# Empty pieces between the products of logits, an opening in another order, and the second head's key copies on VectorE

## The chip, the cores and the metric

The kernel runs on one core of a Trainium2 chip. The metric is the device time of one execution in microseconds (us). Engines go by the names of the profile: PE (TensorE matmul; PEld its weight loads), DVE (VectorE), ACT (ScalarE), POOL (GpSimd) and SP (SyncE, which issues most DMAs). L120 is line 120 of the kernel before. Each engine works through its own instructions in program order, and the kernel sets that order by hand.

## The reference

Attention with two window masks, and a mixture of experts on its output. Shapes: q, k, v are (8, 8, 576, 64); the experts see x of (4608, 512), with 8 experts of 512 x 1024.

```
scores = q @ k^T / 8                      # per batch and head
rel = i - j
plain:   0 <= rel < 32                    # heads 0 to 3
dilated: 0 <= rel < 128 and rel % 4 == 0  # heads 4 to 7
attn = softmax(where(mask, scores, -1e9))
x = (attn @ v), heads side by side        # (4608, 512)

do = x @ w_skip > 0                       # rows that go to an expert
logits = x @ w_gate ; e = argmax ; g = softmax(logits)[e]
out = x + do * g * (relu(x @ w1[e]) @ w2[e])
```

## The kernel before, in words

**Attention in 24 steps.** A quad is two batches and four heads of one kind (plain or dilated); there are 8 quads of 3 parts, so 24 steps. `Attention.run` writes each step's instructions in the order of the string `STEP`, letter by letter, and every engine then keeps that order. Step t works on several steps at once: `A` is the weighted sum (attention times v, L184) of step t, `T` the transposes of the weights (L172) of t+1, `E` the exponential (L157) of t+2, `R` the products of scores (L139) and the three `S` the shift of t+3: add the mask on DVE (L147), row maximum on DVE (L151), subtract it on POOL (L153). `D` normalises (L194, L196, L198 on DVE), `X` transposes the finished rows of the step before (L241 on PE, L244 or L251 on ACT). `k0A` and `k1A` copy the keys of t+4.

**Keys.** `place` (L120) copies the 64 partitions of one head of a pair into one of two block-diagonal tiles `kT`; the other half of each head's block is zero, cleared once at the start by `clear` as listed in `CLEAR` (all four on DVE, L105). A product of scores needs both heads' copies, and the one PSUM tile `s` that the mask's add of the step before has read. In the steps both copies are on ACT; in the opening the first is on ACT and the second on DVE.

**Opening.** Before step 0 a loop over t = 0 to 3 writes: copies of t, products of t, all three parts of its shift, the next load, the exponential of t - 1; and last the transposes of step 0.

**Router.** After each pair of batches but the last, `Router.run` is a generator whose pieces turn x into lists of rows for the experts: four products of logits (L509, each of four matmuls per batch half, in `logits`) with a copy by ACT (L511), nine transposes (L521) with reductions on DVE (L523), `choose`, `rank`, `find`, `put` (L664) for rows and for gates, then `listed`. It is started at the second `X` of the first step of the next pair, and each `w` in `STEP` draws one piece; there are 13 `w` per step. For the third pair, the wrapper `early` does more once it hears `listed`: it closes the first expert's list (L489 and the small DVE rows L491 to L742), gathers its first two tiles of rows (L878 on POOL), writes 16 empty pieces, then the transposes of the gathered rows (L896) and the first three products of the expert's hidden layer (L914). What is left of the pieces after step 23 is drained in one go.

**Experts.** After the attention `finish` routes the last pair while the first expert goes on; then seven more experts follow, each with L914 (up) and L984 (down), the weights split into a high and a low part (L805 on ACT, L806 on DVE or POOL).

Of the kernel before, what the change touches and what calls it, by code (L numbers as in the profile page):

```python
# [20 lines left out]
B, H, S, D = 8, 8, 576, 64  # L21
NTOK, DM = B * S, H * D
E, F = 8, 1024
GQ = 64
NG = S // GQ
W = 32
# [41 lines left out]
class Attention:  # L68
# [27 lines left out]
    def clear(self, tile, hh, eng):  # L96

        dst = tile[64 - 64 * hh:128 - 64 * hh, hh]
        if eng == "A":
            n = 3 * 4  # L100
            dst = dst.rearrange("c n x -> c (n x)").rearrange("c (n x) -> c n x", n=n)
            zeros = self.junk[64 - 64 * hh:128 - 64 * hh, 0:dst.shape[2]]
            self.nc.scalar.copy(out=dst, in_=zeros.unsqueeze(1).broadcast_to(list(dst.shape)))
        else:
            {"V": self.nc.vector, "G": self.nc.gpsimd}[eng].memset(dst, 0.0)  # L105

    def load(self, kind, t):

        src = {"q": self.q, "k": self.k, "v": self.v}[kind][t]
        tile = self.kp.tile([P, 4, src.shape[2]], F32, name=kind, bufs=3 if kind == "q" else 2)  # L110
        n = W + GQ * NB if kind == "k" and t // PARTS % 2 == 0 else src.shape[2]
        self.nc.sync.dma_start(out=tile[:, :, 0:n], in_=src[:, :, 0:n])
        return tile[:, :, 0:n] if kind == "k" else tile.rearrange("c (r b) (g y i) -> c r b g y i", r=2, g=NB, y=2)
# [142 lines left out]
    def run(self, router, experts, early, finish):  # L256


        nc = self.nc
        quads = [(bp, half) for bp in range(B // 2) for half in range(2)]  # L260
        steps = PARTS * len(quads)
        ins, diags, xTs, sms, shifts, exps, pend = {}, {}, {}, {}, {}, {}, {}

        def load(kind, t):
            if t < steps:
                ins[kind, t] = self.load(kind, t)

        def product(t):
            if t < steps:
                i, part = divmod(t, PARTS)  # L270
                sms[t], go, shift, exps[t] = self.scores(quads[i][1], ins["q", t], diags["k", t], part)
                go()
                shifts[t] = shift()

        def shift(t):
            next(shifts.get(t, iter(())), None)

        def exp(t):
            if t < steps:
                exps.pop(t)()  # L280

        def place(t, kind, hh, eng):
            if t < steps:
                diags[kind, t] = self.place(kind, t, ins[kind, t], int(hh), eng)


        masks = make_masks(nc, self.kp)
        for kind, t in FIRST:
            load(kind, t)
        nc.vector.memset(self.junk, 0.0)  # L290
        self.maskp = next(masks)
        for op in CLEAR.split():
            self.clear(self.kts[int(op[1])], int(op[2]), op[3])
        make_identity(nc, self.ident)
        self.maskd = next(masks)
        self.warm(WARM)
        def turn(t):
            if t < steps:
                go, *pend[t] = self.weighted(sms.pop(t))
                go()  # L300

        for t in range(4):
            place(t, "k", 0, "A")
            place(t, "k", 1, "V")
            if t < 3:
                product(t)
                for _ in range(3):
                    shift(t)
                load("k", t + 2)
                if t == 1:  # L310
                    load("q", 3)
            if t in (1, 2):
                exp(t - 1)
        turn(0)

        works, news, stores, xp = [iter(())], [], [], []
        for t in range(steps):
            i, part = divmod(t, PARTS)
            bp, half = quads[i]
            g0 = NB * part  # L320
            while stores:
                self.store_rows(*stores.pop())
            for kind, ahead in (("k", 5), ("q", 4), ("v", 2)):
                if (kind, t + ahead) not in FIRST + FOLLOW:
                    load(kind, t + ahead)
            if t == 1:
                self.prepare()
                dil_rows = make_dil_rows(nc, self.consts["pool"])
                next(dil_rows)
            elif t == 2:  # L330
                self.dil_rows = next(dil_rows)
            if t == WSTART - 1:
                experts.open_first()
            if t == WSTART:
                experts.load_next()
            if half == 0 and part == 0 and bp:
                news.append(early(bp - 1, router(bp - 1, xTs[bp - 1])))
            xh = self.xp.tile([P, NB, 256], F32, name="xh", bufs=3)
            sums, divide = pend.pop(t)
            divides = []  # L340
            for op in STEP.split():
                if op == "T":
                    turn(t + 1)
                elif op == "R":
                    product(t + 3)
                elif op == "E":
                    exp(t + 2)
                elif op == "S":
                    shift(t + 3)
                elif op == "A":  # L350
                    sums(ins["v", t])
                    divides.append(divide(xh))
                elif op == "D":
                    next(divides[0])
                elif op == "X":
                    if xp:
                        xp.pop(0)()
                    if not xp and news:
                        works[0] = news.pop()
                elif op == "W":  # L360
                    if t > WSTART:
                        experts.split_first()
                elif op == "w":
                    next(works[0], None)
                else:
                    place(t + 4, *op)
            if half == 0 and part == 0:
                xTs[bp] = self.xp.tile([P, 4, 2, S], F32, name="xT")
            xp = self.transpose_x(xTs[bp], half, xh, g0)
            stores.append((bp, half, xh, g0))  # L370
        for _ in works[0]:
            pass
        self.att_ctx.close()
        finish(xp, bp, xTs[bp], lambda: self.store_rows(*stores.pop()))
# [13 lines left out]
LATER = 8  # L388
WSTART = 16
GATHER = 16  # L390
WARM = 12
FIRST = [("k", 0), ("q", 0), ("k", 1), ("q", 1), ("v", 0), ("q", 2), ("v", 1)]
FOLLOW = [("k", 2), ("k", 3), ("q", 3), ("k", 4)]
CLEAR = "k00V k01V k10V k11V"

STEP = "E A w T w D w R D w D w X w S w X w S w k0A W w W w k1A W w S w W"
CAP = 384
NT = CAP // P
TILES = [NT] * 5 + [NT - 1] * 3
# [427 lines left out]
class Experts:  # L827
# [189 lines left out]
    def finish(self, e, t, w, hs, th, xg, tag="o"):  # L1017
        r, a = self.router, NT * e + t
        return self.down(w, hs, th, xg[:, t], r.write[:, a:a + 1], r.gate[:, a:a + 1], self.views[t], tag)
# [4 lines left out]
    def early_rows(self):  # L1024

        for _ in range(GATHER):
            yield
# [168 lines left out]
def make_dil_rows(nc, const):  # L1196

    pos = const.tile([P, NG], F32, name="pos")
    res = const.tile([P, NG], F32, name="res")
    rows = const.tile([P, B // 2, NG], F32, name="rowsf")  # L1200
    rows_i = const.tile([P, B // 2, NG], I32, name="rowsi")
    for p in range(0, P, W):
        nc.gpsimd.iota(pos[p:p + W], pattern=[[W, NG]], base=0, channel_multiplier=1,
                       allow_small_or_imprecise_dtypes=True)
    yield
    nc.vector.tensor_scalar(out=res, in0=pos, scalar1=float(RL), scalar2=float(4 - 2 * S), op0=ALU.is_ge, op1=ALU.mult)
    nc.vector.scalar_tensor_tensor(out=res, in0=pos, scalar=float(2 * RES), in1=res, op0=ALU.mult, op1=ALU.add)
    for bp in range(B // 2):
        for p in range(0, P, W):
            b, y = divmod(p // W, 2)  # L1210
            nc.vector.tensor_scalar_add(rows[p:p + W, bp], res[p:p + W], float(2 * S * (2 * bp + b) + 2 * y + 1))
    nc.vector.tensor_copy(out=rows_i, in_=rows)
    yield rows_i
# [3 lines left out]
def moe_attention_kernel(ctx: ExitStack, tc: tile.TileContext, q, k, v, w_skip, w_gate, w1, w2, out):  # L1217
    nc = tc.nc

    def early(bp, listing):  # L1220

        for name in listing:
            if name == "listed" and bp == B // 2 - 2:
                router.close_early()
                router.read_list(0, EARLY)
                experts.xg0 = experts.fetch(0, 0, EARLY, rows=NTOK - 2 * S)
                router.write_list(0, EARLY)
            yield
        if bp == B // 2 - 2:
            yield from experts.early_rows()  # L1230
            yield from experts.early_hidden()
# [120 lines left out]
```

## Time and profile before

| | |
|---|---|
| times of 3 runs | 501.49, 502.75 (median), 507.65 us |
| profiled execution, its own time | 501.86 us |
| its span, first to last instruction | 499.8 us |
| mean granted TensorE clock in the span | 0.922 |
| PE, PEld busy | 413.4 us (83%), 343.2 us (69%) |
| DVE, ACT, POOL busy | 273.7 us (55%), 221.7 us (44%), 158.5 us (32%) |
| HBM read, written | 80.27 MB, 14.94 MB (191 GB/s over the span) |

The span falls into an opening (to 25.68 us, where the first weighted sum starts), the 24 steps (to about 217 us), the routing of the last pair beside the first expert (to about 275 us), and the experts. In a row of the timeline the first number is the start, the second the duration, then engine, line, operation, what it writes and reads, its shape and count; in brackets stands how long the engine was idle before it and what ended that wait. "Issue" means that nothing the profile shows was waited for. The ends of matmuls are modelled.

### The profile page before, as it was taken

To read this page: it belongs to the slowest core of one execution; us is meant where nothing else is said; L and a number is where in the kernel's file an instruction comes from. 1 tells how busy PE (TensorE), PEld (TensorE's weight loads), DVE (VectorE), ACT (ScalarE), POOL (GpSimd) and SP (SyncE) were. 2 spreads that over 40 slices of the span, in tenths; PEclk is the share of its full clock that TensorE was granted. 3 is DMA by queue.
4 is the path that set the end of the run, shared out by engine and by line. 5 is a ranking of instruction groups with operands and counts; after the bars stand their busy time and mean duration, and the time that the engine had idled before them with its cause. 6 is when DMAs were issued, how large, how long until landed. Compare 5 with 4: busy or idle time off the path is not lost. (4 is left out here: it accounts for less than half of the span.)

```text
span 499.8 us, 13402 instructions
## 1 busy us (share of the span) xinstructions
PE 413.4 (83%) x5426; PEld 343.2 (69%) x5426; DVE 273.7 (55%) x575; ACT 221.7 (44%) x441; POOL 158.5 (32%) x217
## 2 busy tenths in 40 slices
PE   5576678787966786668779999999999999999980
PEld 3455554665655555556658988988989989797970
DVE  4477343964586439431966464573573665757620
ACT  2265365646655565324325361452452534645500
POOL 3253352248127673262534042301202113030000
PEclk8698798978999789669999999999999999999995
DMA  8469856969697966271075665446256445755000
GB/s 293 156 206 300 284 198 205 337 231 295 226 325 261 352 217 164 90 228 48 1 232 189 225 220 179 140 168 208 85 171 200 138 162 194 244 206 206 21 26 13
DMA packets 44297, 95.50 MB, mean 191 GB/s; under 512 B 5243, under 2 KB 16395, under 8 KB 44224
## 3 DMA queue, kind: packets, MB, share of 16 engines
q1 hardware_dynamic: 38976, 79.08, 47.6%
q0 software_dynamic: 5248, 15.44, 9.1%
q8 instruction: 46, 0.75, 0.6%
q14 instruction: 27, 0.22, 0.1%
HBM read 80.27 MB, written 14.94 MB: 191 GB/s over the span
## 5 line engine op out<-in xcount | busy, mean ns | idle before, releaser
L984 PE MATMUL o<-w,h 128*128 128x512 f32 x320 | 104.3, 400 | 1.5 <-ACT h L917 1.1
L884 POOL DMA_INDIRECT out_dram<-yo,write x21 | 22.6, 1074 | 160.4 <-DVE yo L989 160.4
L914 PE MATMUL s<-xh,w 128*128 128x384 f32 (+1 forms) x236 | 70.3, 313 | 0.0
L139 PE MATMUL s<-kT,q 128*32 128x128 f32 x1152 | 47.8, 319 | 27.1 <-DVE kT L120 10.7
L914 PE MATMUL s<-xl,w 128*128 128x384 f32 (+1 forms) x236 | 70.0, 311 | 0.0
L984 PEld LDWEIGHTS o<-w,h 128*128 128x128 f32 x320 | 59.1, 188 | 13.9 <-ACT h L917 1.5
L153 POOL TENSOR_TENSOR sm<-sm,mx 128x768 f32<-128x768 f32 x24 | 36.6, 1525 | 94.2 <-DVE mx L151 52.4
L139 PEld LDWEIGHTS s<-kT,q 128*32 128x32 f32 x1152 | 38.3, 128 | 34.8 <-issue 24.9
L917 ACT ACTIVATE h<-s 128x384 fp32r<-128x384 f32 (+1 forms) x59 | 26.2, 444 | 81.1 <-issue 35.4
L184 PE MATMUL o<-v,pT 64*32 64x65 f32 x2304 | 37.0, 237 | 17.7 <-issue 14.2
L184 PEld LDWEIGHTS o<-v,pT 64*32 64x32 f32 x2304 | 28.9, 110 | 26.2 <-issue 19.9
L120 ACT COPY kT<-k 64x1024 f32<-64x1024 f32 (+1 forms) x44 | 43.8, 996 | 5.0 <-DMA k<-in_k_dram 4.5
L914 PEld LDWEIGHTS s<-xh,w 128*128 128x128 f32 x236 | 44.6, 189 | 1.3 <-issue 1.0
L914 PEld LDWEIGHTS s<-xl,w 128*128 128x128 f32 x236 | 44.6, 189 | 0.4
L157 ACT ACTIVATE sm<-sm 128x768 f32<-128x768 f32 x24 | 20.3, 845 | 40.7 <-POOL sm L153 40.5
L806 DVE TENSOR_TENSOR w2l<-w2l,w 128x512 fp32r<-128x512 f32 x40 | 27.6, 691 | 18.6 <-ACT w L805 17.1
L226 POOL DMA_INDIRECT out_dram<-xh,rowsi x33 | 33.5, 1014 | 11.9 <-issue 8.6
L878 POOL DMA_INDIRECT xg<-out_dram,read x24 | 24.4, 1018 | 39.3 <-DMA out_dram<-yo,write 15.1
L806 DVE TENSOR_TENSOR w0l<-w0l,w 128x512 fp32r<-128x512 f32 x40 | 27.7, 691 | 15.1 <-ACT w L805 13.5
L918 DVE SCALAR_TENSOR_TENSOR h<-s,h 128x384 fp32r<-128x384 f32 (+1 forms) x59 | 29.0, 491 | 11.3 <-ACT h L917 11.2
L241 PE MATMUL tp<-ident,xh 128*128 128x128 f32 x144 | 25.9, 314 | 8.9 <-ACT pT L173 8.3
L989 DVE SCALAR_TENSOR_TENSOR yo<-o,gate,xg 128x512 f32<-128x512 f32 x21 | 15.7, 750 | 29.5 <-PE o L984 26.6
(203 smaller groups left out, 758.4 us busy)
## 6 DMA issues: line engine op xcount, KB each, us to landing
v<-in_v_dram SPq DMA_DIRECT2D x24, 780.0 KB
w0l<-in_moe_w_dram SPq DMA_DIRECT2D x48, 256.0 KB
w1l<-in_moe_w_dram SPq DMA_DIRECT2D x40, 256.0 KB
w2l<-in_moe_w_dram SPq DMA_DIRECT2D x40, 256.0 KB
q<-in_q_dram SPq DMA_DIRECT2D x24, 384.0 KB
k<-in_k_dram SPq DMA_DIRECT2D x12, 512.0 KB
k<-in_k_dram SPq DMA_DIRECT2D x12, 448.0 KB
out_dram<-xh SPq DMA_DIRECT2D x24, 192.0 KB
```

What stands on the lines that cost most here:

```text
L120: copy(out=to[own, hh, :, 0:tile.shape[2]], in_=tile[own])
L139: nc.tensor.matmul(ps[0][p:p + W, r, 2 * KW * g:2 * KW * (g + 1)], lhsT=q[:, r, b, g, sub], rhs=kT[:, :, r, b, a:a + KW], start=True, stop ...
L153: nc.gpsimd.tensor_tensor(out=rows, in0=rows, in1=mx.broadcast_to([P, 4 * NB, KW]), op=ALU.subtract)
L184: nc.tensor.matmul(ps[0][p:p + W, hh, y * m:y * (m + 1)], lhsT=pT[own, NB * r + g, p:p + W], rhs=v[own, r, b, g, sub], start=True, stop=True,)
L226: nc.gpsimd.indirect_dma_start(out=self.views[g].rearrange("n (s c) -> (n s) c", s=2), out_offset=bass.IndirectOffsetOnAxis(ap=self.dil_ro ...
L241: nc.tensor.transpose(out=tp[:, P * g:P * g + P], in_=xh[:, g, P * r:P * r + P], identity=self.ident)
L806: (engine or self.nc.vector).tensor_tensor(out=lo, in0=raw, in1=hi.bitcast(F32), op=ALU.subtract)
L878: self.nc.gpsimd.indirect_dma_start(out=xg, out_offset=None, in_=self.out[0:rows], in_offset=bass.IndirectOffsetOnAxis(ap=row, axis=0),)
L914: nc.tensor.matmul(ps[0], lhsT=w(part, k, P * f, P), rhs=x[:, k], start=(i == 0), stop=(i == len(terms) - 1))
L917: nc.scalar.activation(out=hh, in_=ps[0], func=AF.Relu)
L918: return lambda: nc.vector.scalar_tensor_tensor(out=hl, in0=ps[0], scalar=0.0, in1=hh.bitcast(F32), op0=ALU.max, op1=ALU.subtract)
L984: nc.tensor.matmul(ps[0], lhsT=h[:, ts], rhs=w(part, f, 0, DM), start=(i == 0), stop=(i == len(terms) - 1))
```

## The change

Four things, in one function or table each.

- `early` writes three empty pieces after each of the four products of logits, so a product is followed by the next one four `w` later. To make room, whatever is left of an old generator is run to its end before a new one takes its place.
- The opening is written out: keys of steps 0 and 1 first, then products and shifts interleaved, the last exponential at the end.
- `CLEAR` gives the two clears of the second head's tiles to ACT (a copy of zeros, in rows of 512), and two stay on DVE.
- `STEP` has `k1V` for `k1A`: the second head's key copy moves from ACT to DVE in the steps as well.

```
         if eng == "A":
-            n = 3 * 4
+            n = 2
...
-        for t in range(4):
+        def keys(t):
             place(t, "k", 0, "A")
             place(t, "k", 1, "V")
-            if t < 3:
-                product(t)
-                for _ in range(3):
-                    shift(t)
-                load("k", t + 2)
-                if t == 1:
-                    load("q", 3)
-            if t in (1, 2):
-                exp(t - 1)
+
+        keys(0)
+        keys(1)
+        load("k", 2)
+        load("q", 3)
+        load("k", 3)
+        product(0)
+        shift(0)
+        product(1)
+        shift(0)
+        shift(0)
+        shift(1)
+        keys(2)
+        load("k", 4)
+        product(2)
+        exp(0)
+        shift(1)
+        shift(1)
         turn(0)
+        shift(2)
+        keys(3)
+        shift(2)
+        shift(2)
+        exp(1)
...
                     if not xp and news:
+                        for _ in works[0]:
+                            pass
                         works[0] = news.pop()
...
+SPREAD = 3
...
-CLEAR = "k00V k01V k10V k11V"
+CLEAR = "k00V k01A k10V k11A"
 
-STEP = "E A w T w D w R D w D w X w S w X w S w k0A W w W w k1A W w S w W"
+STEP = "E A w T w D w R D w D w X w S w X w S w k0A W w W w k1V W w S w W"
...
         for name in listing:
+            if name and name.startswith("logits"):
+                for _ in range(SPREAD):
+                    yield
             if name == "listed" and bp == B // 2 - 2:
```

What this moves is seen in the order of the instructions. The lines of the changed kernel are 17 to 20 higher from the router on (L509 is L526 there, L489 is L506, L896 is L913).

DVE in the opening, from its first instruction on; `kT_83` and `kT_84` are the two tiles of keys, `s` the scores, `sm` and `mx` the masked scores and their maxima. Before:

```order
L290 MEMSET junk 128x256
L1182 COPY maskp<-near 128x1152
L1182 COPY maskd<-near 128x1152
L105 MEMSET kT_83 64x1024 x2
L105 MEMSET kT_84 64x1024 x2
L120 COPY kT_83<-k 64x4x224
L147 TENSOR_TENSOR sm<-s,maskp 128x768
L151 TENSOR_REDUCE mx<-sm 128x12
L120 COPY kT_84<-k 64x4x224
L147 TENSOR_TENSOR sm<-s,maskp 128x768
```

And now:

```order
L1199 COPY maskd<-near 128x1152
L105 MEMSET kT_83 64x1024
L105 MEMSET kT_84 64x1024
L120 COPY kT_83<-k 64x4x224
L120 COPY kT_84<-k 64x4x224
L147 TENSOR_TENSOR sm<-s,maskp 128x768
L151 TENSOR_REDUCE mx<-sm 128x12
L147 TENSOR_TENSOR sm<-s,maskp 128x768
L120 COPY kT_83<-k 64x4x224
L151 TENSOR_REDUCE mx<-sm 128x12
```

Two clears have left DVE, the second tile's keys are copied before the first scores are masked, and the second mask comes ahead of the third copy.

PE where the router of the first pair starts (`lt` are the logits, `xT` the transposed rows, `wg` the gate's weights). Before:

```order
L139 MATMUL s<-kT_84,q 32x128 x24
L241 MATMUL tp<-ident,xh 128x128 x6
L509 MATMUL tp<-xT,wg 32x288 x16
L521 MATMUL tp<-ident,lt 128x128 x8
L184 MATMUL o<-v,pT 32x65 x48
L521 MATMUL tp<-ident,lt 128x128
L172 MATMUL tp<-ident,sm 128x128 x6
L139 MATMUL s<-kT_83,q 32x128 x24
```

And now:

```order
L241 MATMUL tp<-ident,xh 128x128 x6
L526 MATMUL tp<-xT,wg 32x288 x8
L184 MATMUL o<-v,pT 32x65 x48
L172 MATMUL tp<-ident,sm 128x128 x6
L526 MATMUL tp<-xT,wg 32x288 x4
L139 MATMUL s<-kT_83,q 32x128 x24
L241 MATMUL tp<-ident,xh 128x128 x3
L526 MATMUL tp<-xT,wg 32x288 x4
L241 MATMUL tp<-ident,xh 128x128 x3
L538 MATMUL tp<-ident,lt 128x128 x9
```

Half of the logits still stand together; the other half is split around the next scores, and the transposes of the logits follow a whole step later. Every later piece of the router comes 12 `w`, nearly one step, later.

PE at the end of the last step, after the last transposes of attention weights (`rhs` and `oneh` are the gates' list, `count` the rows per expert, `xg` the gathered rows). Before:

```order
L664 MATMUL w<-rhs_3333,oneh 128x72
L489 LDWEIGHTS ones
L489 MATMUL w<-count,ones 128x1
L184 MATMUL o<-v,pT 32x65 x48
L241 MATMUL tp<-ident,xh 128x128 x6
L896 MATMUL tp<-ident,xg 128x128 x8
```

And now:

```order
L184 MATMUL o<-v,pT 32x65 x48
L241 MATMUL tp<-ident,xh 128x128 x3
L681 LDWEIGHTS oneh
L681 MATMUL w<-rhs_3413,oneh 128x72
...
L241 MATMUL tp<-ident,xh 128x128 x3
L506 LDWEIGHTS ones
L506 MATMUL w<-count,ones 128x1
L913 MATMUL tp<-ident,xg 128x128 x8
```

The count that closes the first expert's list stood ahead of the last weighted sums; now it stands behind them, and PE's next instructions are the transposes of the rows that are gathered only after it.

## The prediction

> **What bounds the kernel now.** I read the time of each stage first, then what PE waits for in the steps, then the timeline at the places that the change touches. The busy time of each engine by stage (start:end, length, then busy us and instructions of PE, PEld, DVE, ACT, POOL, the granted clock, the busy share of the DMA engines, GB/s):
>
> ```profile
> 25.68:212.00 186.32, 138.99 (x3698) 105.12 (x3698) 109.86 (x250) 104.19 (x196) 82.87 (x106) 0.87 0.74 248
> 212.00:219.00 7.00, 3.53 (x105) 2.45 (x105) 2.37 (x12) 0.99 (x4) 4.65 (x14) 0.74 0.46 120
> ...
> 275.00:499.80 224.80, 209.63 (x1164) 187.70 (x1162) 118.91 (x206) 88.19 (x183) 39.62 (x46) 0.98 0.47 156
> ```
>
> The experts from 275 us on are PE alone: 209.6 of 224.8 us busy. The change touches nothing there. Whatever it is worth arises before 219 us and is carried through. In the 24 steps no engine is full: PE is busy for 75%, DVE 59%, ACT 56%, DMA 74%, and PE's clock is 0.87. So a step is set by who waits for whom on PE, which the groups of PE in the window of the steps (25 to 216 us) show; after the bar stand busy us, mean ns, the idle time before the group and what ended it:
>
> ```profile
> L139 PE MATMUL s<-kT,q 128*32 128x128 f32 x1008 | 39.7, 306 | 16.8 <-issue 7.8 <-ACT kT L120 6.4 <-DMA q<-in_q_dram 2.1
> L184 PE MATMUL o<-v,pT 64*32 64x65 f32 x2304 | 37.0, 237 | 17.7 <-issue 14.2 <-DVE xh L198 1.7 <-ACT pT L173 1.2
> L241 PE MATMUL tp<-ident,xh 128*128 128x128 f32 x138 | 25.1, 316 | 8.9 <-ACT pT L173 8.3 <-issue 0.5
> ```
>
> PE idles 16.8 + 17.7 + 8.9 = 43.4 us before these three. The largest part, 7.8 + 14.2 + 0.5 = 22.5 us, is "issue", for which no engine is named; the change doesn't address it. What it can address is 6.4 us for ACT's key copies and 8.3 + 1.2 us for ACT's copies of transposed weights.
>
> **The opening: a gain of 4.5 us.** The timeline:
>
> ```profile
> 5.12 0.94 ACT L120 COPY kT<-k 64x896 f32<-64x896 f32 x1 [2.92 <-DMA k<-in_k_dram]
> ...
> 7.48 0.91 DVE L105 MEMSET kT<- 64x1024 f32 x1 [0.25 <-issue]
> 7.68 0.94 ACT L120 COPY kT<-k 64x896 f32<-64x896 f32 x1 [1.61 <-DMA k<-in_k_dram]
> 8.64 0.91 DVE L105 MEMSET kT<- 64x1024 f32 x1 [0.25 <-issue]
> 9.58 0.62 DVE L120 COPY kT<-k 64x896 f32<-64x896 f32 x1
> ...
> 10.31 2.79 PE L139 MATMUL s<-kT,q 128*32 128x128 f32 x48 [4.43 <-DVE kT L120]
> 13.22 0.96 DVE L147 TENSOR_TENSOR sm<-s,maskp 128x768 f32<-128x768 f32 x1 [3.01 <-issue]
> ...
> 15.19 0.62 DVE L120 COPY kT<-k 64x896 f32<-64x896 f32 x1
> 15.32 1.83 POOL L153 TENSOR_TENSOR sm<-sm,mx 128x768 f32<-128x768 f32 x1 [8.02 <-DVE mx L151]
> ...
> 16.08 2.72 PE L139 MATMUL s<-kT,q 128*32 128x128 f32 x48 [2.98 <-DVE kT L120]
> ...
> 21.72 2.57 PE L139 MATMUL s<-kT,q 128*32 128x128 f32 x48 [2.92 <-DVE kT L120]
> ...
> 24.21 1.44 PE L172 MATMUL tp<-ident,sm 128*128 128x128 f32 x6
> 25.68 0.35 PE L184 MATMUL o<-v,pT 64*32 64x65 f32 x16
> ```
>
> Each of the three products waits 3 to 4.4 us for DVE's key copy. The first copy stands behind four clears; two go to ACT, which sat idle for 2.92 us before its first copy. A clear is 64x1024 elements, as ACT's key copies of 1.05 us below are: two make 2.1 us, inside the 2.92. (A copy of zeros with a type change isn't in the trace; at twice the price ACT's first copy would end at 7.4, still before DVE's.) So DVE's first copy moves from 9.58 up by 9.58 - 7.48 = 2.1 us, and the first product to 8.2. From there with the same durations: product to 11.0, mask from 11.1 (0.1 us after it, as 13.22 is after 13.10) to 12.1; the second copy is made by 8.8, since those keys had landed by 7.68, so the second product runs from 12.2 to 14.9, its mask to 16.0, the third copy to 16.7, the third product from 16.8 to 19.4, the transposes from 19.4 (the first exponential is done by 16) and the first sums at 19.4 + 1.47 = 20.9 for 25.68: 4.8 us earlier. The third keys' load is now issued at 8.2 for 10.29 and landed by 15.19 before, so by 13.1. I take 4.5. Bounds: 2.1 if only the first product keeps its lead, 5.3 if no DVE row lies between.
>
> **The logits: a gain of 1.5 us.** An empty piece issues nothing, and the generator with 12 more pieces still ends within the 78 that six steps draw, so that the new drain finds nothing left for the first pairs. What counts is the order. The second of the three places where a router starts:
>
> ```profile
> 126.08 4.74 PE L509 MATMUL tp<-xT,wg 128*32 128x288 f32 x32
> ...
> 130.75 1.09 PE L521 MATMUL tp<-ident,lt 128*128 128x128 f32 x8
> 131.78 1.18 PE L184 MATMUL o<-v,pT 64*32 64x65 f32 x96
> ...
> 133.80 1.52 PE L139 MATMUL s<-kT,q 128*32 128x128 f32 x48
> ...
> 136.05 1.28 PE L184 MATMUL o<-v,pT 64*32 64x65 f32 x96
> ```
>
> Between 126.08 and 137.33 PE has no gap of a microsecond: 4.74 us of logits are work, not waiting. Split, they let the next scores start earlier: half the logits (2.4), the sums (1.2), transposes (0.9) and a quarter (1.2) give 131.8 for 133.80, so 2.0 us. But the other quarter and the logits' transposes (2.3 us) still come before the following sums, which can't start earlier than 136. What is left is the lead that DVE, POOL and ACT get on the next scores. I take 0.5 us at each of three places; bounds: 2.0 earlier three times (6), and 1.0 later three times, where the transposes wait for ACT's last copy.
>
> **The key copies on DVE: nothing, with wide bounds.**
>
> ```profile
> 136.70 0.94 DVE L151 TENSOR_REDUCE mx<-sm 128x12 f32<-128x768 f32 x1
> 136.79 2.11 ACT L120 COPY kT<-k 64x1024 f32<-64x1024 f32 x2
> ...
> 137.82 1.47 POOL L153 TENSOR_TENSOR sm<-sm,mx 128x768 f32<-128x768 f32 x1 [8.34 <-PE tp L172]
> ...
> 138.01 1.32 DVE L689 CAST vals<-gates 128x9 bf16<-128x9 f32 x1
> ...
> 138.95 1.52 PE L139 MATMUL s<-kT,q 128*32 128x128 f32 x48 [0.53 <-ACT kT L120]
> ```
>
> ACT loses 1.05 us in each of 20 steps, DVE gains 0.62. The new copy stands behind the row maximum, just where POOL starts to subtract. Two rows say what that does. In the opening the copy started first (15.19) and POOL's subtraction, begun at 15.32, took 1.83 us for 1.47. At 138.01 POOL was first and a cast of 9 elements took 1.32 us on DVE, to 139.33, just after POOL ended (139.29). In 11 of the 20 steps the copy follows the maximum directly: keys are ready 0.7 us after it for 1.26 before (138.90 against 137.64), 0.5 us sooner, and POOL is some 0.4 late. In the other 9, rows of the router stand between: the copy waits out the subtraction and is ready 0.2 + 1.47 + 0.62 = 2.3 us after the maximum, 1.0 us later than before, and the normalisation queued behind it on DVE is late too. Where PE doesn't wait for keys, none of this counts. Gain and loss are of one size; I take 0. Bounds: a gain of 6.4, all of PE's waits for ACT's copies, and a loss of 9 x 1.0 = 9.
>
> The Trainium skill, "SBUF — State Buffer", section "Who interferes with whom", has the rule for this: DVE and GpSimd share a pair of ports, a DVE copy in its two-port mode and a GpSimd instruction exclude each other, and whoever issues first holds it for the whole instruction. Both rows above agree in kind, though 1.83 is shorter than 0.5 us of blocking and 1.47 of work in full. By that rule alone, with the copy second everywhere, this term would be a loss; its time stands with the rivals.
>
> **The end of the steps: a loss of 3 us.**
>
> ```profile
> 201.47 0.55 PE L241 MATMUL tp<-ident,xh 128*128 128x128 f32 x3 [3.28 <-ACT pT L173]
> ...
> 211.90 0.16 PE L489 MATMUL w<-count,ones 128*128 128x1 bf16 x1 [0.32 <-DVE at_gates L667]
> 212.00 1.44 PE L184 MATMUL o<-v,pT 64*32 64x65 f32 x89
> ...
> 213.13 0.99 POOL L878 DMA_INDIRECT xg<-out_dram,read  x1 [6.35 <-DVE write L740]
> 214.43 0.97 POOL L878 DMA_INDIRECT xg<-out_dram,read  x1 [0.30 <-issue]
> ...
> 216.16 4.04 SPq L796 DMA_DIRECT2D w1l<-in_moe_w_dram  x8
> ...
> 216.60 0.96 DVE L198 TENSOR_TENSOR xh<-o,z 128x768 f32<-128x768 f32 x1
> ...
> 218.89 0.93 PEld L896 LDWEIGHTS tp<-ident,xg 128*128 128x128 f32 x5 [2.27 <-DMA xg<-out_dram,read]
> ```
>
> From the count (211.90) to the landing of the second gather (218.89) are 7.0 us. Before, the last sums, transposes and normalisation lie in these; PE still idles for 2 us. Now the count comes behind the last normalisation, which ends at 216.60 + 0.96 = 217.6: with 7.0 us more the rows land at 224.6, 5.7 later, and everything on PE is queued behind them, the last pair's routing too. Some comes back: the same pieces of router delayed the last steps (the wait of 3.28 us in the first row is behind them on DVE, POOL and ACT), and they now lie a step later. I set 2.7 against the 5.7, so 3. Bounds: 0 if that wait and as much again vanish, 7 if nothing comes back and the weight loads at 216.16, which were behind the gathers and are now ahead, delay them by 1.3 us, a gather's own spacing.
>
> **The sum**: -4.5 - 1.5 + 0 + 3 = -3.0, from the profiled execution's 501.86 to 498.9. The median of the runs is 502.75, 0.9 higher; I give 499.
>
> **Rivals.** First, PE's waits go altogether: keys 6.4 and weights 8.3 + 1.2, 15.9 us. For it speaks that both chains run through ACT, which loses a copy per step; against it that the copies of weights wait behind the exponential and that behind POOL, which gains nothing. With two thirds of it, 10.6, on top of the opening and the end: 501.86 - 4.5 - 10.6 + 3 = 489.8.
>
> Second, slower: DVE's copies wait for POOL. Place: the 9 steps with router rows between maximum and copy, at 1.0 us, and 0.4 us of late subtraction in the other 11. All of it on PE's path is 13.4: 501.86 - 4.5 - 1.5 + 3 + 13.4 = 512.3; the 9 steps alone 507.9. It decides from a loss of 3.0 us on, three of the nine steps. For it speaks the cast at 138.01, against it that PE waited for keys in these steps for only half a microsecond (0.53).
>
> Third, the gather is the whole price: the end costs 7 and the logits give nothing: 501.86 - 4.5 + 7 = 504.4. For it speaks that PE has nothing else queued there; against it the wait of 3.28 us.
>
> **How the numbers follow.** The forecast has a chance of 0.5, the first rival 0.2, the second 0.17, the third 0.13. Two per cent, about what a measurement of this kernel can tell from no change, is 10 us: 492.7 and 512.8. Faster by more comes from most of the first rival (0.15) and a little of the forecast (0.03): 0.18. Slower by more comes from the second where its 512.3 is passed: 0.06. Within: 0.76. The range of 489 to 508 takes in the first rival's figure and the second's nine steps.
>
> **What would show it.** Right: the first sums near 21 us; products of scores with shorter waits after ACT's copies and some after DVE's; POOL's subtractions near 1.8 us beside DVE's copies; the stretch from the first sums to the last as long as before within 3 us; a PE gap of 4 to 7 us before L913, with the gathers issued behind the last normalisation. Wrong: first sums later than 23; that stretch shorter by over 6 us (then PE's waits fell with ACT's load); or DVE waiting more than 10 us beside POOL.

## The result and the profile after

| | before | after |
|---|---|---|
| median of 20 runs each, one chip | 501.28 us | 505.38 us |
| lowest to highest | 496.35 to 507.65 us | 500.60 to 508.91 us |
| profiled execution, its span | 501.86, 499.8 us | 504.88, 503.2 us |

The ratio is 1.0073, with a 95% interval of 1.0044 to 1.0101: the change makes the kernel slower by 4 us where 3 to 4 us of gain were forecast. A few executions of every kernel are longer than the rest; ratios, and all differences between two kernels below, are taken without them. The busy time by stage after has the columns of the prediction's table; the stages are the opening, the steps, the end of the steps up to the first expert product, and the experts. In the changed kernel the gathers are L895 (L878 before), the expert's products L931 (L914) and the weight loads L813 (L796).

```profile
0.00:21.95 21.95, 11.91 (x162) 7.45 (x162) 9.20 (x12) 7.31 (x8) 7.74 (x31) 0.85 0.75 256
21.95:212.26 190.31, 141.35 (x3785) 104.47 (x3785) 120.78 (x269) 85.50 (x178) 89.27 (x109) 0.88 0.72 245
212.26:224.07 11.81, 4.18 (x25) 3.18 (x25) 3.36 (x15) 2.19 (x7) 4.64 (x14) 0.50 0.75 255
...
278.00:503.20 225.20, 209.70 (x1164) 187.79 (x1162) 119.00 (x206) 88.18 (x183) 40.81 (x46) 0.98 0.47 155
```

The same cuts of before, beside which the first three rows are to be read:

```profile
0.00:25.68 25.68, 13.95 (x162) 9.55 (x162) 11.03 (x14) 7.09 (x8) 8.53 (x31) 0.73 0.64 219
25.68:214.78 189.10, 141.04 (x3794) 106.76 (x3795) 110.88 (x259) 104.19 (x196) 84.22 (x108) 0.87 0.73 244
214.78:220.63 5.85, 3.05 (x15) 1.96 (x15) 2.18 (x5) 2.11 (x7) 4.28 (x14) 0.65 0.82 231
```

Opening 25.68 to 21.95 (-3.7), steps 189.1 to 190.3 (+1.2), end 5.85 to 11.81 (+6.0): together +3.4, the difference of the two spans. ACT's busy time in the steps fell by 18.7 us and DVE's rose by 9.9, near what 20 moved copies make up, and the steps became no shorter. PE's groups in the steps say that a wait changed its name:

```profile
L139 PE MATMUL s<-kT,q 128*32 128x128 f32 x1008 | 39.3, 298 | 17.6 <-issue 6.4 <-DVE kT L120 6.1 <-ACT pT L173 2.2
L184 PE MATMUL o<-v,pT 64*32 64x65 f32 x2304 | 38.9, 246 | 14.9 <-issue 12.6 <-ACT pT L173 1.3 <-DMA v<-in_v_dram 0.5
L241 PE MATMUL tp<-ident,xh 128*128 128x128 f32 x133 | 25.4, 317 | 7.9 <-ACT pT L173 7.9
```

The wait for ACT's keys was 6.4 us; the wait for DVE's is 6.1. The three groups idle 40.4 us for 43.4, and others take that back: PE idles 190.31 - 141.35 = 49.0 us in the steps, 48.1 before. The opening after:

```profile
7.17 1.30 DVE L120 COPY kT<-k 64x896 f32<-64x896 f32 x2
...
7.89 1.52 PE L139 MATMUL s<-kT,q 128*32 128x128 f32 x48 [1.83 <-DVE kT L120]
...
10.59 1.52 PE L139 MATMUL s<-kT,q 128*32 128x128 f32 x48 [1.18 <-issue]
...
16.69 0.62 DVE L120 COPY kT<-k 64x896 f32<-64x896 f32 x1 [3.57 <-DMA k<-in_k_dram]
16.77 0.94 ACT L120 COPY kT<-k 64x896 f32<-64x896 f32 x1 [8.00 <-DMA k<-in_k_dram]
...
17.76 2.79 PE L139 MATMUL s<-kT,q 128*32 128x128 f32 x48 [5.65 <-ACT kT L120]
...
21.95 0.47 PE L184 MATMUL o<-v,pT 64*32 64x65 f32 x16
```

The first two products come where they were put or earlier; the third now waits 5.65 us for ACT's copy, and that copy had waited for the transfer of the keys. And the end of the steps:

```profile
212.33 3.65 SPq L813 DMA_DIRECT2D w1l<-in_moe_w_dram  x8
...
212.77 0.96 DVE L198 TENSOR_TENSOR xh<-o,z 128x768 f32<-128x768 f32 x1
...
214.11 0.21 PE L506 MATMUL w<-count,ones 128*128 128x1 bf16 x1
...
215.41 0.99 POOL L895 DMA_INDIRECT xg<-out_dram,read  x1 [4.99 <-DVE write L757]
...
221.70 0.45 PE L913 MATMUL tp<-ident,xg 128*128 128x128 f32 x1 [7.38 <-DMA xg<-out_dram,read]
...
224.07 0.56 PE L931 MATMUL w<-xh,w 128*128 128x256 f32 x1
```

The last normalisation is 3.8 us earlier than before (212.77 for 216.60), the gather 2.3 later (215.41 for 213.13), and PE has nothing to do for 7.4 us before the rows' transposes. One pair of profiles would thus put the whole loss at the end. The runs below put the price of the late gather at about half of the 6.0 us.

### The profile page after: what moved, and what is told of

Read it like the earlier page. It is cut to its first block, busy times and chain, and to the rows that moved or that the text cites. A ratio compares the mean times of both kernels' runs of the same rounds, so it can differ in the third digit from the quotient of the medians.

```text
span 503.2 us, 13406 instructions
## 1 busy us (share of the span) xinstructions
PE 412.9 (82%) x5426; PEld 340.0 (68%) x5426; DVE 283.1 (56%) x593; ACT 203.3 (40%) x423; POOL 162.2 (32%) x217
## 5 line engine op out<-in xcount | busy, mean ns | idle before, releaser
L931 PE MATMUL s<-xh,w 128*128 128x384 f32 (+1 forms) x236 | 70.4, 313 | 0.0
L931 PE MATMUL s<-xl,w 128*128 128x384 f32 (+1 forms) x236 | 70.0, 311 | 0.0
L153 POOL TENSOR_TENSOR sm<-sm,mx 128x768 f32<-128x768 f32 x24 | 37.7, 1570 | 91.2 <-DVE mx L151 44.8
L139 PE MATMUL s<-kT,q 128*32 128x128 f32 x1152 | 45.1, 301 | 26.3 <-DVE kT L120 7.9
L934 ACT ACTIVATE h<-s 128x384 fp32r<-128x384 f32 (+1 forms) x59 | 26.1, 443 | 80.7 <-issue 35.4
L139 PEld LDWEIGHTS s<-kT,q 128*32 128x32 f32 x1152 | 36.7, 121 | 31.7 <-issue 17.3
L184 PE MATMUL o<-v,pT 64*32 64x65 f32 x2304 | 38.9, 246 | 14.9 <-issue 12.6
L931 PEld LDWEIGHTS s<-xh,w 128*128 128x128 f32 x236 | 44.6, 189 | 1.3 <-issue 1.0
L931 PEld LDWEIGHTS s<-xl,w 128*128 128x128 f32 x236 | 44.6, 189 | 0.4
L895 POOL DMA_INDIRECT xg<-out_dram,read x24 | 25.7, 1069 | 36.7 <-DMA out_dram<-yo,write 14.5
L935 DVE SCALAR_TENSOR_TENSOR h<-s,h 128x384 fp32r<-128x384 f32 (+1 forms) x59 | 29.0, 491 | 10.8 <-ACT h L934 10.7
L241 PE MATMUL tp<-ident,xh 128*128 128x128 f32 x144 | 27.5, 319 | 7.9 <-ACT pT L173 7.9
L915 ACT CAST xh<-tp 128x256 fp32r<-128x256 f32 (+1 forms) x32 | 13.6, 426 | 45.2 <-PE tp L913 43.8
```

Of the source, the lines that this page charges most:

```text
L139: nc.tensor.matmul(ps[0][p:p + W, r, 2 * KW * g:2 * KW * (g + 1)], lhsT=q[:, r, b, g, sub], rhs=kT[:, :, r, b, a:a + KW], start=True, stop ...
L153: nc.gpsimd.tensor_tensor(out=rows, in0=rows, in1=mx.broadcast_to([P, 4 * NB, KW]), op=ALU.subtract)
L184: nc.tensor.matmul(ps[0][p:p + W, hh, y * m:y * (m + 1)], lhsT=pT[own, NB * r + g, p:p + W], rhs=v[own, r, b, g, sub], start=True, stop=True,)
L241: nc.tensor.transpose(out=tp[:, P * g:P * g + P], in_=xh[:, g, P * r:P * r + P], identity=self.ident)
L895: self.nc.gpsimd.indirect_dma_start(out=xg, out_offset=None, in_=self.out[0:rows], in_offset=bass.IndirectOffsetOnAxis(ap=row, axis=0),)
L931: nc.tensor.matmul(ps[0], lhsT=w(part, k, P * f, P), rhs=x[:, k], start=(i == 0), stop=(i == len(terms) - 1))
```

## The experiments

Each group of runs had one chip and the kernel before beside it (the second, third and fifth group had the same chip): medians of all executions of before were 492.19 us (first group), 500.48 (second), 502.19 (third), 492.66 (fourth) and 501.77 (fifth). Ratios are against the kernel before of the same group, with 95% intervals. Differences in us between kernels of one group are of medians; most are uncertain by 2 to 3 us either way. The edits are shown against the changed kernel; no run leaves out any of the computation.

### First group: each part alone, and the third pair

e1: empty pieces for the routers of the first two pairs only.

```
-            if name and name.startswith("logits"):
+            if name and name.startswith("logits") and bp < B // 2 - 2:
```

> The changed kernel, but the logits of the third pair follow each other without empty pieces, so its list is closed ahead of the last weighted sums again. Theory (the end): in the changed profile every step is some 3 to 4 us ahead of before and the last normalisation ends 3.8 us earlier, and all is lost between it and the first product of the first expert, because the rows are gathered only behind the last step. Then this kernel keeps the opening's 3.8 us and has no loss at the end: 501.3 - 3.8 = 497.5, the count some 4 us before its 211.9, and PE's gap before the transposes of the gathered rows back at 2 to 3 us. Rival (the steps): empty pieces or VectorE's key copies cost time in the steps, and the end is only where it shows; then at least half of the 4.1 us that the changed kernel lost stays, 503 or more.

e2 is the kernel before with the empty pieces and the run to the end of an old generator; nothing else of the change.

> The kernel before with the three empty pieces after each product of logits, and nothing else. Theory (the end): the steps take as long as before and the end loses the 7.3 us that the two profiles show between the last normalisation and the first expert: 501.3 + 7.3 = 508.6, a PE gap of 6 to 8 us ahead of the transposes of the gathered rows. Rival (an early step wakes the loss): the loss at the end is due to the weight loads that the earlier opening lets in ahead of the gathers; then it is smaller here, 504 or less.

e3 is the opening with its clears; `SPREAD = 0` in effect, `k1A` for `k1V` in `STEP`.

> The kernel before with the opening and the clears of the change, and nothing else. Theory: the first weighted sums start at 21.9 us for 25.7 and the lead is kept to the end: 501.3 - 3.8 = 497.5. Rival (the lead is eaten): the steps wait for transfers and for what the profile calls issue, so that a lead of the opening is gone by the end: 501.

e4 is the kernel before with `k1V` for `k1A` in `STEP`.

> The kernel before with the second head's keys copied by VectorE in the steps, and nothing else. Theory: PE's waits for keys change their name and not their size (6.1 us for VectorE where 6.4 us were for ScalarE in the two profiles): 501.3, within 1 us. Rival (VectorE and GpSimd hold each other up): subtractions of 1.8 us beside the copies put 0.4 us into eight or more steps: 504 or more. Rival (ScalarE is relieved): 498 or less.

Measured: e1 1.0017 (0.9979 to 1.0055), e2 1.0033 (0.9996 to 1.0070), e3 0.9860 (0.9795 to 0.9926), e4 1.0030 (0.9994 to 1.0067). The opening alone is worth more than was forecast. The other two alone cost about 1.5 us each, with intervals that reach down to nothing, and with the third pair's pieces taken out the opening's gain still doesn't come back. So the late gather isn't the only price, and the parts don't add up. In e2's profile the rows' gather comes 6.5 us after the last sums although the opening is the old one, so the expectation's rival, that the earlier opening makes the loss at the end, isn't borne out, though its time is.

### Second group: the parts in pairs

e5: `SPREAD = 0`. e6: `k1A` for `k1V`. e7: `k1A`, and pieces for the first two pairs as in e1. e8: the change unaltered.

> The whole change, but with SPREAD = 0, so that the logits run in one piece as before and the third pair's routing ends where it did. Theory A (the gather that comes behind the last normalisation is the whole loss, and the opening alone is worth 1.4%): without it this is as fast as the opening alone, 0.984 to 0.988 of before, and the rows' transposes start within 2 us after the last sums. Theory B (DVE's key copies undo the opening, since they lengthen the steps once the opening no longer leads): 0.996 to 1.004, with the stretch from the first to the last sums 4 us or more longer than in the kernel with the opening alone.

> The whole change, but with the second head's keys still copied by ACT. Theory A (the late gather is the whole loss): as slow as the whole change, 1.004 to 1.010, with a gap of 5 us or more on PE before the rows' first transpose. Theory B (DVE's copies undo the opening): 0.986 to 0.992, the opening's 1.4% less what the spread alone cost (0.3%), though the gap before the rows' transpose is there.

> Opening as in the change, keys on ACT, empty pieces only for the routers of the first two pairs. Both theories have the gather early here. If spreading the logits shortens the steps at all (a gain of up to 3.6 us was read from the profile of the kernel with the spread alone), this beats the opening alone: 0.978 to 0.984. If spreading is worth nothing, as predicted to within 1.5 us for three places, it equals the opening alone, 0.984 to 0.988.

> The change unaltered, on the chip of the other three. Expected at 1.004 to 1.010 of before, with first sums near 22 us, the last normalisation 2 us or more before the rows' gathers and 5 to 8 us of idle PE before the rows' first transpose. If it comes out at 0.995 or below here, the loss differs from chip to chip and no part of the change can be named for it from one chip alone.

Measured: e5 0.9925 (0.9890 to 0.9959), e6 1.0007 (0.9977 to 1.0036), e7 0.9936 (0.9899 to 0.9973), e8 1.0124 (1.0071 to 1.0177). Neither theory holds alone: the loss with ACT's copies and the late gather (e6) is smaller than A says and larger than B says, e5 lies between the two as well, e7, expected at 0.988 or below either way, is slower than that, and e8 is a little above the 1.010 set for it. What the third pair's pieces cost with ACT's copies is the difference of e6 and e7, 499.80 - 496.97 = 2.8 us. In the timeline of e6 the gather stands behind the last normalisation:

```profile
208.69 0.96 DVE L198 TENSOR_TENSOR xh<-o,z 128x768 f32<-128x768 f32 x1
210.03 0.21 PE L506 MATMUL w<-count,ones 128*128 128x1 bf16 x1
211.33 0.99 POOL L895 DMA_INDIRECT xg<-out_dram,read  x1 [4.01 <-DVE write L757]
...
217.48 0.45 PE L913 MATMUL tp<-ident,xg 128*128 128x128 f32 x1 [7.24 <-DMA xg<-out_dram,read]
```

and in that of e7 ahead of it, with a wait of 0.85 us in the place of 7.24:

```profile
201.19 0.16 PE L506 MATMUL w<-count,ones 128*128 128x1 bf16 x1 [0.32 <-DVE at_gates L684]
202.41 0.99 POOL L895 DMA_INDIRECT xg<-out_dram,read  x1 [6.24 <-DVE write L757]
...
205.86 0.96 DVE L198 TENSOR_TENSOR xh<-o,z 128x768 f32<-128x768 f32 x1
205.90 0.45 PE L913 MATMUL tp<-ident,xg 128*128 128x128 f32 x1 [0.85 <-DMA xg<-out_dram,read]
```

In all profiles the first expert product comes 7 to 11 us after the gather. What the third pair's pieces move is the gather against the end of the last sums: from between 1.7 us ahead and 0.7 behind to 3.1 to 7.7 behind.

### Third group: where VectorE makes its copy

e9 is e5 (no empty pieces) with the copy ahead of the scores' mask; e10 is e3, e11 is e7 and e12 is e5 again.

```
-... D w X w S w X w S w k0A W w W w k1V W w S w W"
+... D w X w k1V S w X w S w k0A W w W w W w S w W"
```

> Opening of the change, logits in one piece, the second head's keys on VectorE as in the change, but the copy stands ahead of the scores' mask in each step instead of behind the row maximum (k1V moved ahead of the S that masks). VectorE waits there for the product of scores anyway (3.1 us in one step of the kernel with the opening and the copies), and GpSimd's subtraction is half a step away. Theory B (the copy behind the maximum costs, because it meets the subtraction and the router's rows): no subtraction above 1.7 us, and 0.4 to 0.9% less time than opening and copies with the copy in its place. Theory C (what counts is only that ACT has a copy fewer; where VectorE makes it is of no account): within 0.3% of opening and copies.

> The opening alone again, now beside the others on one chip: keys on ACT, logits in one piece. Theory B: 0.983 to 0.990 of before, and at least 0.4% below opening and copies. If it comes out within 0.3% of opening and copies, the copies cost nothing, as predicted, and the two kernels differed before only because they ran on two chips.

> Opening, keys on ACT, and empty pieces in the routers of the first two pairs, beside the opening alone on one chip. As predicted (spreading is worth between -6 and +3 us, likeliest -1.5 for three places, so -1.0 for two): 0.2% below the opening alone. Theory D (spreading costs by itself, with the gather early): 0.4% or more above the opening alone.

> Opening and VectorE's copies behind the maximum, logits in one piece, beside the same kernel with the copies elsewhere and with ACT's copies. Theory B: 0.990 to 0.996 of before and 0.4% or more above the opening alone; prediction: equal to the opening alone within 0.3%.

Measured: e9 0.9814 (0.9770 to 0.9858), e10 0.9890 (0.9842 to 0.9938), e11 0.9876 (0.9830 to 0.9922), e12 0.9877 (0.9831 to 0.9924). Without empty pieces the copies behind the maximum cost what ACT's cost (497.0 for 496.2 us): "0" was right there. It was right as a balance: the same copies ahead of the mask bring 5.0 us (492.0). So of theory B the place holds, and that the copies cost against ACT's doesn't. The pieces of two pairs cost nothing to be seen with ACT's copies (e11 and e10 are equal within 2.7 us), so theory D isn't borne out. e9 is the best version of the study, 1.9% below before.

### Fourth group: empty pieces beside VectorE's copies

e13 is e1 again; e14 is e13 with the copy ahead of the mask (the edit of e9); e15 the whole change with that edit; e16 has pieces for the third pair alone (`bp == B // 2 - 2` in the line of e1).

> The change with the third pair's empty pieces left out, so the gather comes early. Theory E (the third pair's place is the whole loss): 0.986 to 0.993 of before, as opening and copies. Theory F (the first two pairs' empty pieces cost too where VectorE has the copies): 0.996 to 1.004, with 48 us or more of idle PE between the first and the last sums.

> The same, and VectorE's copies stand ahead of the mask. Theory F, with the copies' place as its cause: 0.980 to 0.987, like opening and copies ahead of the mask (0.981), and idle PE between the sums under 44 us. Theory E: equal to the run before this less the 0.6% that the place was worth without empty pieces.

> The whole change with VectorE's copies ahead of the mask. Theory F: the late gather's 0.8% is left on top of 0.981 to 0.985, so 0.988 to 0.994, with the gather 3 us or more behind the last sums. Theory E (all of the loss, 2%, sits at the third pair): 1.000 or above.

> The change with empty pieces for the third pair's router alone; opening, copies behind the maximum. Theory E: as slow as the whole change, 1.005 to 1.012. Theory F: opening and copies plus the late gather, 0.996 to 1.000, with the gather 3 us or more behind the last sums.

Measured: e13 1.0128 (1.0048 to 1.0208), e14 0.9932 (0.9880 to 0.9983), e15 0.9989 (0.9937 to 1.0040), e16 0.9970 (0.9926 to 1.0015). Three of the four ratios lie above those expected. On this chip before itself was spread from 485.5 to 497.3 us (and one execution of 647.9), so the ratios to it are less certain than the differences within the group; medians of all executions give 1.003, 0.989, 0.995 and 0.992. Among themselves, the copies' place is worth 494.2 - 486.2 = 8.0 us beside the pieces, the third pair's pieces 489.8 - 486.2 = 3.6 us, and the third pair's alone are 5.6 us cheaper than the first two's (488.6 and 494.2). Theory E falls with e13 and e16. Of theory F it is borne out that the first two pairs' pieces cost something beside VectorE's copies; that the copies' place is the cause of that isn't. e14 was to come out at 0.987 or below and stands at 0.9932, 0.0118 above e9, the same kernel without the pieces on another chip. That is some 6 us, uncertain by 3, and no less than the pieces cost with the copies behind the maximum. The idle of PE between the first and the last sums is 44.5 us in e13, where 48 or more was set, and 42.4 in e14, where under 44 was. What the place costs can be seen in e13:

```profile
102.51 0.95 DVE L151 TENSOR_REDUCE mx<-sm 128x12 f32<-128x768 f32 x1
...
103.64 1.47 POOL L153 TENSOR_TENSOR sm<-sm,mx 128x768 f32<-128x768 f32 x1 [2.85 <-DVE mx L151]
103.69 1.43 DVE L641 TENSOR_TENSOR count<-count,cnt 128x8 bf16<-128x8 bf16 x1
105.05 0.82 DVE L673 TENSOR_TENSOR rhs<-at,vals 128x648 bf16<-128x648 bf16 x1
...
105.90 0.62 DVE L120 COPY kT<-k 64x896 f32<-64x896 f32 x1
...
106.62 1.65 PE L139 MATMUL s<-kT,q 128*32 128x128 f32 x48 [2.01 <-DVE kT L120]
```

The maximum is done at 103.46 and the keys at 106.52. Between them the router's count, an addition of 8 elements a row, takes 1.43 us and ends with POOL's subtraction (105.12 and 105.11); the copy stands behind it and one more router row, and PE waits 2.01 us. The same place in e14:

```profile
98.14 1.47 POOL L153 TENSOR_TENSOR sm<-sm,mx 128x768 f32<-128x768 f32 x1 [1.32 <-DVE cnt L639]
98.19 1.45 DVE L641 TENSOR_TENSOR count<-count,cnt 128x8 bf16<-128x8 bf16 x1
...
100.52 1.52 PE L139 MATMUL s<-kT,q 128*32 128x128 f32 x48
...
101.74 0.69 DVE L120 COPY kT<-k 64x1024 f32<-64x1024 f32 x1
```

The count is held up just as long, but the keys were copied beforehand, and the product starts without a wait. POOL's subtractions are the other side (min, median and max in ns); e13, then e14:

```profile
L153 POOL TENSOR_TENSOR sm<-sm,mx x24: 1467/1477/1883, 11.8 to 192.6; 128x768 f32<-128x768 f32 x24
```

```profile
L153 POOL TENSOR_TENSOR sm<-sm,mx x24: 1467/1472/1489, 11.6 to 185.9; 128x768 f32<-128x768 f32 x24
```

Six of the 24 are over 1.7 us in e13, none in e14. The scores' products from the seventh normalisation to the nineteenth, where the routers of the first two pairs run, wait for keys 7.6 us in e13 and not at all in e14:

```profile
L139 PE MATMUL s<-kT,q 128*32 128x128 f32 x576 | 25.3, 319 | 14.1 <-DVE kT L120 7.6 <-issue 4.0 <-ACT pT L173 1.7
```

```profile
L139 PE MATMUL s<-kT,q 128*32 128x128 f32 x576 | 22.6, 295 | 8.4 <-issue 8.1 <-DMA q<-in_q_dram 0.2
```

That window of e13 and e14 by engine:

```profile
61.69:162.31 100.62, 76.82 (x2014) 57.38 (x2013) 68.29 (x151) 46.77 (x98) 42.72 (x48) 0.88 0.79 272
```

```profile
59.76:152.65 92.89, 73.55 (x2014) 55.23 (x2013) 67.36 (x150) 45.62 (x96) 39.72 (x43) 0.87 0.86 297
```

PE idles 100.62 - 76.82 = 23.8 us in e13 and 19.3 in e14. The same difference, length less PE's busy time, in nineteen of the twenty profiles (all but e18's):

| second head's keys | no pieces in these routers | with empty pieces |
|---|---|---|
| ACT | 21.0, 19.4, 23.6: mean 21.3 | 18.3, 20.9, 18.6, 20.0: mean 19.5 |
| DVE behind the maximum | 21.0, 20.7, 25.5, 23.0, 22.0: mean 22.4 | 26.1, 24.4, 24.0, 23.8: mean 24.6 |
| DVE ahead of the mask | 16.4 | 19.3, 19.5: mean 19.4 |

(ACT: before, e3, e10; e2, e6, e7, e11. Behind: e4, e5, e12, e16, e17; after, e1, e8, e13. Ahead: e9; e14, e15.) With ACT's copies empty pieces take 1.8 us of idle away. With DVE's behind the maximum they add 2.2, and with DVE's ahead of the mask about 3, where only one profile has no pieces. So the pieces go with more idle wherever DVE makes its copies. Nor is the increase named for the keys: over PE's groups in these windows, the idle that the profile puts down to DVE's key copies is 7.7 us on average without the pieces and 7.3 with them (behind the maximum), while "issue" grows from 10.8 to 14.2 us, ahead of the mask from 10.8 to 16.9, and with ACT's copies only from 12.1 to 12.8.

### Fifth group: the first two pairs' pieces side by side

e17 is e5 and e18 is e1, again.

> Opening, VectorE's copies behind the maximum, no empty pieces; beside the next run. 0.987 to 0.993 of before, idle PE of 20 to 25 us in the twelve steps from the seventh normalisation to the nineteenth, 7 to 9 us of it waiting for VectorE's keys.

> The same with empty pieces for the routers of the first two pairs. Theory F (empty pieces let the scores come earlier, and then they wait for VectorE's late keys): 0.8% or more above the run before this. Theory G (the two parts add up; the empty pieces are worth 0.1%, as they were with ACT's copies): within 0.3% of the run before this.

Measured: e17 0.9923 (0.9890 to 0.9956), e18 0.9952 (0.9914 to 0.9991): 499.4 against 497.0 us, 2.4 more, with intervals that overlap. G's 0.3% is well within them on this chip, and F's 0.8% at their edge. On the other two chips the same kernel stood at 1.0017 and 1.0128.

## Why the prediction was wrong

Ratios of equal kernels put together (each weighted by the inverse square of its interval) give the parts in the order in which they are added, at 500 us to the whole:

| kernel | ratio, runs it is from | step | forecast |
|---|---|---|---|
| opening | 0.9880 (e3, e10) | -6.0 us | -4.5 |
| and DVE's copies | 0.9914 (e5, e12, e17) | +1.7 | 0 |
| and pieces of two pairs | 1.0000 (e1, e13, e18) | +4.3 | -1.0 |
| and of the third: the change | 1.0084 (result, e8) | +4.2 | +2.5 |

The sum is +4.2 where -3.0 was forecast. Intervals of such ratios are 1 to 2 us wide on either side, so a step is uncertain by 2 us or so, and the third row scatters between chips from 0.995 to 1.013, so its size is the least certain.

**The opening** was right in its steps and small by 1.5 us. The first product came at 7.89 for 8.2, the first sums at 19.0 to 21.95 in the seventeen profiles with it, 25.2 to 25.7 in the three without; 20.9 was forecast. The means are 20.6 and 25.5, so 4.9 us earlier for the 4.8 worked out. One step failed without harm: the third keys were to land by 13.1 and landed at 16.7. What made up for part of it in this profile was luck: the stage ran at a granted clock of 0.85 for 0.73, and its first two products took 1.52 us each for 2.79 and 2.72 (the third took 2.79 again).

**The copies alone** were right, as a balance of gain and loss: +0.8 (e12 against e10) and +1.7 us where 0 stood. Both sides are now measured. Copies moved to DVE and placed ahead of the mask gain 4.2 us (e9 against e10), and the place behind the maximum loses 5.0 (e12 against e9). The mechanism of the second rival, copies that wait out POOL's subtraction behind router rows, is what the rows of e13 show, and a change of place alone removes it; the nine copies behind router rows are ready 2.2 us after the maximum in e12, for 2.3 forecast. Net of the gain it doesn't reach the 3.0 us from which that rival was to decide, until the empty pieces come to it (4.0 us, e8 against e6).

**The logits are the step that failed**: "I take 0.5 us at each of three places", a gain of 1.0 us for the first two pairs. In the change the pieces of these two pairs cost 4.3 us. The term was worked out on the trace of before, where ACT makes the copies. There the runs don't contradict it: e11 equals e10, and idle falls by 1.8 us, though e7 and e11 put together stand at 0.9912, 1.6 us above the opening. With DVE's copies PE's idle rises instead. What was missing is a term for the two edits together, and a term for each edit, each priced against the kernel before, can't show it. Three pairs of kernels, each pair on one chip, bear this out: the copies cost 4.0 us beside all the pieces (e8 against e6) and 0.8 without any (e12 against e10), and the two edits together put e1 6.8 us above e3 (which has few executions), where in the third group each of them alone added under 1 us to the opening. The bound of +9 for the copies was wide enough; that of +3 for the spread, meant for three pairs, doesn't hold the 4.3 of two. Nor are DVE's copies the whole loss: with ACT's copies and all the pieces (e6) the kernel is no faster than before, some 6 us above the opening, where 1.5 was forecast for the pieces and the late gather together.

Why the two together cost is not settled. One thing that the pieces do can be read from the rows. In four steps of each of these two routers, some of its rows stand between the maximum and the copy. There the keys are ready 2.4, 3.1, 2.3 and 0.8 us after the maximum's end without the pieces (e12), and 2.2, 2.3, 3.3 and 3.1 with them (the change), where 2.3 was forecast for each. In sum (8.64 and 10.87 us) that is 2.2 us later for a router and 4.5 for two, as much as the step of the table. But PE's waits named for DVE's keys are as long without the pieces (7.3 us in e5, 8.9 in e12) as with them (6.1 after, 7.6 in e13), and idle rises with copies ahead of the mask too, so it isn't shown that PE pays for this delay.

**The end of the steps** was right in its sum: +3 was forecast, and e6 against e7 and e15 against e14 have +2.8 and +3.6. Its split into 5.7 lost and 2.7 that "comes back" wasn't tested by a run of its own. The stretch from the last sums to the first expert product is 9.1 us on average in the fourteen profiles with an early gather and 13.3 in the six with a late one, so 4.2 longer. The pair of profiles shows +6.0, since that of before has a short end (5.85 us from the last sums to the first expert product; the other profiles with an early gather have 5.7 to 11.1). The rival that the gather is the whole price has the figure nearest to what was measured, 504.4 us, but not the reason: the late gather costs 2.8 to 3.6 us of its 7, and e1 and e13, which have it early, are no faster than before (e18 is, by 0.5%). The first rival (PE's waits go with ACT's copy) falls with e12, which is no faster than the opening alone; even another place for the copy, e9, brings only 4.2 of its 10.6 us.

**What was to show it** came true almost throughout: first sums at 21.95, waits behind DVE's copies, subtractions of 1.8 us, steps as long within 3 us, gathers behind the last normalisation; only the gap of 7.4 us is over the 4 to 7. These signs could not tell -3 from +4, since each was checked within an allowance as large as the sum.

## What to carry to other kernels

Price the edits of a change in pairs where they touch one queue: here a copy moved to DVE and empty pieces that shift the router's rows on DVE each cost little alone, and some 4 us more together. A copy moved to another engine is best placed where that engine waits anyhow, here ahead of the mask, and not behind the instruction that releases POOL's subtraction: place alone was worth 5 to 8 us, more than the choice of the engine (0.8 us behind the maximum). And let the pieces of an early router end before the last step if a gather hangs on them.

## What was not expected of the hardware

An addition of 8 elements a row on DVE takes 0.16 us with POOL issuing transfers, in the timeline of the changed kernel,

```profile
208.14 0.16 DVE L641 TENSOR_TENSOR count<-count,cnt 128x8 bf16<-128x8 bf16 x1
```

and 1.43 to 1.45 beside POOL's subtraction, to the end of that. The Trainium skill, "SBUF — State Buffer", section "Who interferes with whom", says that a DVE instruction with two inputs in SBUF contends with a GpSimd instruction that reads it; these rows agree. So it isn't only copies that are held up there, and whatever is queued behind such a row is late with it.

PE's busy time for the same steps differs between profiles by more than any part of the change is worth, and the granted clock with it. From first to last sums, in e11 and then e15:

```profile
21.10:208.21 187.11, 144.42 (x3795) 106.94 (x3795) 110.74 (x259) 105.12 (x198) 82.58 (x107) 0.85 0.73 247
```

```profile
19.57:190.46 170.89, 129.18 (x3785) 96.64 (x3785) 120.71 (x269) 85.02 (x178) 85.61 (x107) 0.92 0.80 270
```

144.4 and 129.2 us of work for PE at 0.85 and 0.92 granted. So one profile of each of two kernels doesn't show a difference of 4 us; medians side by side on one chip and groups of profiles do.
